# One list-scheduled attention and MLP kernel: filler matmuls at the start, score pieces two by two, batch-0 transposes in separate PSUM slots, and two v tiles ahead of the rest

## The chip, the cores and the metric

The kernel runs on one core of a Trainium2 chip. The metric is device time in microseconds (us), the lower the better. A kernel is timed in several executions; medians are quoted. A ratio is the mean time of one kernel's fast runs over the mean of the other's fast runs in the same rounds, so it is not quite the ratio of the medians quoted beside it. The record's verdict on a kernel is "faster" or "slower" only where the ratio is clear of 2%.

## The reference, cut to what matters

```python
B, H, S, Nb, D = 8, 8, 576, 16, 64          # batches, heads, tokens, beacon keys, head size
k_all = concat([beacon_k, k], axis=2); v_all = concat([beacon_v, v], axis=2)
scores = q @ k_all.T / sqrt(D)              # causal mask on the non-beacon keys
x = softmax(scores) @ v_all                 # -> (B*S, H*D) = (4608, 512)
h = x @ w_in                                # (512, 2048)
out = (relu(h) ** 2) @ w_out                # (2048, 512)
```

Eight batches of attention feed one two-layer MLP. The MLP works on nine chunks of 512 tokens. A batch has 576 tokens, so chunk 3 (tokens 1536 to 2047) needs the first 320 tokens of batch 3, and chunk 4 needs the first 256 of batch 4. Batches and chunks are counted from 0.

## The kernel before

The kernel is not written as a loop. Its Python code makes a list of operations with dependences, priorities and assumed durations, plays them on a small model of the engines, and emits the instructions in the order that comes out. Only the order enters the program. Each engine gets its list in that order, with semaphore waits for the dependences. In what follows "the plan" is that list scheduler.

PSUM is cut into four slots. Each operation that writes PSUM takes one, with a limit for each class:

```python
order = Order(pools={"ps": range(4), "stg": range(NSTG), "pt": range(NPT)},
              limits={"strip": 2, "av": 2, "mlp": 2, "tp": 1})
# in Order.run: an operation is not issued while its class is at its limit or no slot is free
```

A head pair's scores are made in four pieces in the batches after the first (batch 0 is cut differently). Each piece takes one slot, and one ScalarE exponential empties it:

```python
for i, (mms, off, width) in enumerate(ph.pieces):
    ...
    qk = add(f"qk{p}.{n}.{i}", "PE", 0.05 + cols / 2400.0, emit_qk, prio=base + i,
             deps=qk_deps + [take_pt], take=("ps", "strip"), gate=gate)
    ...
    exps.append(add(f"exp{p}.{n}.{i}", "ACT", 0.18 + 2 * width / 1200.0, emit_exp,
                    prio=base + i, deps=[qk], give=qk))
```

Score matmuls contract over 64 rows, and those of two heads run side by side (in the trace of before their starts are 0.003 us apart); value matmuls and MLP matmuls use 128 rows (64*128 against 128*128 in the timeline). After masking, the value matmuls and the normalisation write `xn`, the attention output of a batch. For batches 2 to 7 five DMA transposes per batch turn it into `xT`, which the MLP reads. They are issued on SyncE's queue, together with the fp32 loads of later batches, the q/k transposes of batches 3 to 7 and the stores.

```python
def add_trans(b, x, prio):        # q/k transposes of batch b, on SyncE
    ...
    deps = [cast[b, x, c] for c in range(NT)]                       # all loads cast
    deps += [o for p in range(HP * (b - 2), HP * (b - 1)) for o in qk_ops[p]]   # qT/kT buffer free
    trans[b, x] = [add(f"tr{b}{x}", "SP", 3.8, emit, prio=prio, deps=deps, dma=3.2)]

def add_xt(b):                    # xT of batch b, on SyncE
    for t in range(NT):
        ...
        deps = [norm_ops[HP * b + i, 0] for i in range(HP)] + ring_deps(tok, tok + n)
        o = add(f"xt{b}.{t}", "SP", 1.32, emit, prio=-50.0 + b, deps=deps, dma=0.64 * n / 128)
```

At the start, batch 0's q and k are loaded pair by pair and transposed on TensorE, k and q of a pair into one slot. VectorE copies k out and ScalarE or VectorE q. The v tiles are loaded after the first q has landed, and the MLP's weights after v tile 3.

The softmax here doesn't subtract the row's maximum and nothing guards it: scores larger than these inputs give would overflow.

## Time and profile before

| reading | value | where it is read |
|---|---|---|
| time, median | 355.3 us (354.6 to 355.4) | timed runs |
| TensorE busy | 334.7 of 353.2 us | busy table of the page |
| first MLP matmul, last matmul ends | 27.61, 348.49 us | timeline |
| first exponential | 10.15 us | timeline |
| TensorE waits over 0.9 us after the start | one, 1.0 us | list of waits |

From the page of the kernel before: the busy table, and the rows of TensorE, ScalarE and the granted TensorE clock in 40 slices of the span, each digit a share in tenths.

```profile
PE 334.7 (95%) x2943; PEld 178.6 (51%) x2980; DVE 148.9 (42%) x287; ACT 193.4 (55%) x233; POOL 85.5 (24%) x132
...
PE   3789999999999989999999999999999999999994
...
ACT  2686786287555764665745663676634405505602
...
PEclk9999999999999999999999999999999999999999
```

TensorE is nearly always busy after the third slice. The clock row reads full throughout, but the timeline of all engines says otherwise for the first 23 us. Its columns are start, time, engine, source line, operation, output and input.

```profile
4.63 1.43 PE L405 MATMUL ps<-ident,qk_area 96*64 96x96 bf16 x24 [0.24 <-DMA qk_area<-in_k_dram]
...
10.15 1.54 ACT L520 ACTIVATE pt<-ps 128x736 bf16<-128x736 f32 x2
...
27.61 0.99 PE L678 MATMUL ps<-xT,w_in 128*128 128x240 bf16 x8
...
34.61 0.70 PE L405 MATMUL ps<-ident,qk_area 96*64 96x96 bf16 x24
```

The same 24 transposes take 1.43 us at 4.6 us (a wait of up to 0.24 us for the q load is in it; the next pair's take 1.31 us) and 0.70 us at 34.6 us, so TensorE starts at about half its later speed. The first exponential starts at 10.15 us and the first MLP matmul at 27.61 us.

The list of waits of TensorE (what it waited for, total us, times, longest):

```profile
PE ps L401 <- DVE bks L373: 4.2, 1, 4.2
...
PE ps L506 <- DMA kT<-qk_area: 1.0, 1, 1.0
PE ps L550 <- DVE pt L530: 0.9, 1, 0.9
...
PE ps L678 <- ACT qT L280: 0.6, 1, 0.6
```

After the start there is one wait of 1.0 us for the key transposes of batch 4 (at 129 us) and one of 0.6 us.

A score island (a run of score or transpose matmuls between others; it has two edges, entry and exit), in TensorE's timeline:

```profile
203.53 1.91 PE L678 MATMUL ps<-xT,w_in 128*128 128x256 bf16 x16
205.37 0.58 PE L506 MATMUL ps<-qT,kT 64*128 64x496 bf16 x4
205.88 1.38 PE L678 MATMUL ps<-xT,w_in 128*128 128x256 bf16 x11
```

Sixteen matmuls of 256 columns start 0.109 us apart, which is 1.744 us. The scores start 1.84 us after the first of them, so 0.096 us is lost on entering. Leaving costs about the same: 0.09 us, the median of 68 exits in this trace.

### The profile page before, as it was taken

Reading aid. Unit: us, or ns where it says so; the run is one execution under the profiler, and the core shown is the slowest. Engines: PE = TensorE matmul, PEld = TensorE weight load, DVE = VectorE, ACT = ScalarE, POOL = GpSimd, SP = SyncE. Lnnn points to the kernel's source line nnn. Section 1 sums busy time; section 2 is a strip of 40 time slices with the busy share of each in tenths; the row PEclk is TensorE's granted clock in tenths of the full one; section 3 lists DMA queues with packets and bytes.
Section 4 is the critical chain, followed back from the end, with each engine's and each line's share of the span. In section 5 each row is a group of like instructions: output and inputs, shape, how many; then the busy total and the mean of one; then the engine's idle time right before and its main releaser. Section 6 shows DMA issues by size and latency. Waiting matters only on the chain.

```text
span 353.2 us, 7173 instructions
## 1 busy us (share of the span) xinstructions
PE 334.7 (95%) x2943; PEld 178.6 (51%) x2980; DVE 148.9 (42%) x287; ACT 193.4 (55%) x233; POOL 85.5 (24%) x132
## 2 busy tenths in 40 slices
PE   3789999999999989999999999999999999999994
PEld 2459665554545444444446874445454444444441
DVE  5576674349714455146622753247132302301300
ACT  2686786287555764665745663676634405505602
POOL 7273721209215504133501651000000000000000
PEclk9999999999999999999999999999999999999999
DMA  7999999965969999699989999440013103003003
GB/s 101 183 160 204 223 206 211 201 169 118 206 116 236 223 221 191 138 224 222 251 137 202 248 213 209 115 118 11 0 61 69 59 0 121 0 0 121 0 0 119
DMA packets 137008, 49.49 MB, mean 140 GB/s; under 512 B 123344, under 2 KB 132048, under 8 KB 136976
## 3 DMA queue, kind: packets, MB, share of 16 engines
q1 hardware_dynamic: 127472, 40.09, 53.4%
q0 software_dynamic: 9504, 8.95, 15.7%
q8 instruction: 23, 0.38, 0.5%
q14 instruction: 9, 0.07, 0.1%
HBM read 37.22 MB, written 9.44 MB: 132 GB/s over the span
## 4 chain that ended last, share of the span: by engine, by line
PE 74%; DMA 12%; SPq 5%; ACT 4%; DVE 2%; issue 2%; POOL 1%; ACTq 0%; DVEq 0%; POOLq 0%
PE ps L678 32%; PE ps L718 27%; PE ps L550 7%; PE ps L506 6%; DMA stg<-in_k_dram 4%; DMA stg<-in_v_dram 4%; SPq L597 3%; ACT pt L520 2%; DMA kT<-qk_area 2%; DMA stg<-in_q_dram 1%; SPq L327 1%; DVE kT L282 1%; DMA qk_area<-in_q_dram 1%; PE ps L405 1%; ACT qT L280 1%
## 5 line engine op out<-in xcount | busy, mean ns | idle before, releaser
L678 PE MATMUL ps<-xT,w_in 128*128 128x512 bf16 (+3 forms) x689 | 131.9, 340 | 1.6 <-ACT qT L280 0.6
L718 PE MATMUL ps<-w_out,g 128*128 128x512 bf16 x554 | 129.5, 380 | 1.4 <-issue 0.5
L520 ACT ACTIVATE pt<-ps 128x832 bf16<-128x832 f32 (+4 forms) x128 | 105.3, 865 | 40.7 <-PE ps L506 40.2
L678 PEld LDWEIGHTS <-w_in 128*128 128x128 bf16 x704 | 66.0, 98 | 57.6 <-issue 6.0
L694 ACT ACTIVATE g<-ps 128x1024 bf16<-128x1024 f32 (+2 forms) x65 | 61.8, 951 | 54.0 <-PE ps L678 53.8
L718 PEld LDWEIGHTS <-g 128*128 128x128 bf16 x576 | 53.0, 98 | 65.7 <-issue 5.8
L703 DVE TENSOR_TENSOR g<-g 128x1024 bf16<-128x1024 bf16 (+2 forms) x80 | 53.0, 664 | 77.5 <-ACT g L694 77.0
L530 DVE TENSOR_TENSOR pt<-pt,tri 128x1024 bf16<-128x1024 bf16 (+1 forms) x36 | 24.8, 692 | 50.1 <-ACT pt L520 48.6
L282 POOL CAST qk_area<-stg 128x512 bf16<-128x512 f32 (+2 forms) x50 | 34.6, 704 | 35.0 <-DMA stg<-in_k_dram 18.7
L282 POOL CAST vb<-stg 128x512 bf16<-128x512 f32 (+1 forms) x38 | 26.0, 695 | 69.6 <-DMA stg<-in_v_dram 59.1
L506 PE MATMUL ps<-qT,kT 64*128 64x80 bf16 (+6 forms) x400 | 39.1, 291 | 1.7 <-DMA kT<-qk_area 1.0
L280 ACT COPY osb<-ps 128x1024 f32<-128x1024 f32 (+1 forms) x19 | 18.3, 969 | 40.6 <-PE ps L718 40.3
L550 PEld LDWEIGHTS <-pt 128*128 128x128 bf16 (+1 forms) x960 | 34.5, 99 | 8.8 <-issue 2.5
L550 PE MATMUL ps<-vb,pt 128*128 128x65 bf16 (+1 forms) x960 | 36.5, 196 | 1.9 <-DVE pt L530 0.9
L566 DVE TENSOR_TENSOR xn<-ps,rcp 128x640 bf16<-128x640 f32 (+2 forms) x36 | 27.0, 750 | 1.7 <-DMA xT<-xn 0.4
L506 PEld LDWEIGHTS <-kT 64*128 64x128 bf16 x400 | 13.7, 97 | 24.2 <-issue 18.8
L565 DVE RECIPROCAL rcp<-ps 128x10 f32<-128x10 f32 (+2 forms) x36 | 7.6, 211 | 38.1 <-PE ps L550 36.2
L696 DVE TENSOR_SCALAR g<-ps 128x1024 bf16<-128x1024 f32 (+2 forms) x15 | 15.8, 1053 | 7.8 <-PE ps L678 7.0
L280 ACT COPY qT<-ps 128x576 bf16<-128x576 bf16 x12 | 7.7, 640 | 16.1 <-DVE kT L282 13.0
L282 DVE COPY kT<-ps 128x16 bf16<-128x16 bf16 (+1 forms) x24 | 9.9, 456 | 9.7 <-PE ps L405 7.5
L405 PE MATMUL ps<-ident,qk_area 96*64 96x96 bf16 x288 | 11.1, 233 | 2.9 <-DMA qk_area<-in_k_dram 1.8
L534 DVE TENSOR_TENSOR pt<-pt,tri 80x160 bf16<-80x160 bf16 x32 | 10.8, 339 | 0.0
(31 smaller groups left out, 57.1 us busy)
## 6 DMA issues: line engine op xcount, KB each, us to landing
out_dram<-osb SPq DMA_DIRECT2D x17, 512.0 KB, 3.5
stg<-in_v_dram SPq DMA_DIRECT2D x21, 256.0 KB, 5.1
stg<-in_q_dram SPq DMA_DIRECT2D x20, 256.0 KB, 4.8
stg<-in_k_dram SPq DMA_DIRECT2D x15, 256.0 KB, 5.1
w_in<-in_moe_w_in_dram POOLq DMA_DIRECT2D x4, 512.0 KB, 8.2
w_out<-in_moe_w_out_dram POOLq DMA_DIRECT2D x4, 512.0 KB, 10.6
stg<-in_v_dram SPq DMA_DIRECT2D x7, 224.0 KB, 4.7
qk_area<-in_k_dram POOLq DMA_DIRECT2D x4, 288.0 KB, 12.4
```

What stands on the lines that cost most here:

```text
L280: nc.scalar.copy(dst, src)
L282: eng[e].tensor_copy(dst, src)
L506: nc.tensor.matmul(st[:, hj, at:at + t1 - t0], kT[b % 2][hp, pr, 128 * c:128 * c + 128], qT[b % 2][hp, pr, t0:t1], start=True, stop=True,)
L520: nc.scalar.activation(pt[take_pt.held[2]][:, :, off:off + width], st[:, :, 0:width], AF.Exp, bias=0.0, scale=scale)
L530: nc.vector.tensor_tensor(out=d, in0=d, in1=tri[:, m0:m0 + m, :][:, None].to_broadcast([128, 2, m, 128]), op=ALU.min)
L550: nc.tensor.matmul(a[:, hj, (t - tl[0]) * (D + 1):(t - tl[0] + 1) * (D + 1)], P[0:rr, hj, o:o + 128], vb[b % 2][0:rr, c, h, :], start=(c = ...
L566: nc.vector.tensor_tensor(out=xn[b % 2].rearrange("p t (h d) -> p h t d", d=D)[:, 2 * pr:2 * pr + 2, tl[0]:tl[0] + nt], in0=a[:, :, :, 0:D ...
L678: nc.tensor.matmul(h[:, u, lo - spans[0][0]:hi - spans[0][0]], w_in_sb[:, mc, ft * 128:(ft + 1) * 128], xT[:, mc, lo % RING:lo % RING + hi ...
L694: nc.scalar.activation(dst, h, AF.Relu, bias=0.0, scale=1.0)
L696: nc.vector.tensor_scalar(out=dst, in0=h, scalar1=0.0, scalar2=None, op0=ALU.max)
L703: nc.vector.tensor_tensor(out=d, in0=d, in1=d, op=ALU.mult)
L718: nc.tensor.matmul(o[:, ts, :], G[:, fc, (2 * u + ts) * 128:(2 * u + ts + 1) * 128], w_out_sb[:, fc, :], start=(fc == 0), stop=(fc == NFT ...
```

## The change

It has four parts. The first three are meant to bring the first MLP unit forward; the last is meant to save changes between MLP and score matmuls (0.096 us on entering in the trace of before).

1. Filler matmuls on TensorE, into the slot that the next operation will use, wherever the plan has a gap before the first MLP unit: 79 in all, 40 of them before the first transpose.
2. In batch 0, k and q of a pair are transposed into slots of their own, and ScalarE alone copies q. (The class limit of these transposes becomes 2, for all batches.)
3. v tiles 0 and 1 are loaded at once; tiles 2 to 4 wait for the third pair's q; the weights wait for v tile 2 instead of 3.
4. In batches 3 to 7 score pieces are made two by two: one operation takes two PSUM slots and issues both pieces back to back; the two exponentials give the slots back one at a time. The assumed duration of a score operation gains 0.12 us, in all batches.

The diff, cut to its core:

```diff
-                            pool, cls = op.take
-                            if not self.pools[pool]:
+                            pool, cls, n = op.take if len(op.take) == 3 else op.take + (1,)
+                            if len(self.pools[pool]) < n:
                                 continue
-                            if cls in self.limits and self.inuse[cls] >= self.limits[cls]:
+                            if cls in self.limits and self.inuse[cls] + n > self.limits[cls]:
                                 continue
 ...
+    filler = pt[NPT - 1][:, 0, 1920:2048]
+    nc.vector.memset(filler, 0.0)
+    def keep_busy(slot, gap):
+        for _ in range(int((gap - 0.15) / 0.07)):
+            nc.tensor.matmul(ps[slot][:, 0, 0:128], filler, filler, start=True, stop=True)
 ...
+            for part in (("k", "q") if b == 0 else ("kq",)):
 ...
+    QGROUP = lambda b: 1 + (b >= 3)
 ...
-        for i, (mms, off, width) in enumerate(ph.pieces):
+        for i in range(0, len(ph.pieces), QGROUP(b)):
+            group = ph.pieces[i:i + QGROUP(b)]
 ...
-            qk = add(f"qk{p}.{n}.{i}", "PE", 0.05 + cols / 2400.0, emit_qk, prio=base + i,
-                     deps=qk_deps + [take_pt], take=("ps", "strip"), gate=gate)
+            qk = add(f"qk{p}.{n}.{i}", "PE", 0.17 + cols / 2400.0, emit_qk, prio=base + i,
+                     deps=qk_deps + [take_pt], take=("ps", "strip", len(group)), gate=gate)
 ...
-            w_ops["in", i] = add(... sync=[v_loads[0][3]] if i == 0 else (), ...)
+            w_ops["in", i] = add(... sync=[v_loads[0][2]] if i == 0 else (), ...)
 ...
-                if c == 0:
-                    sync = [strided[0][0, "q"]]
+                if c == 2:
+                    sync = [strided[0][2, "q"]]
```

More of the change, by code (lines that the diff above doesn't have):

```diff
@@ L21 @@
                  "take", "give", "gate", "held", "dma", "pe_time", "behind", "followers",
-                 "sync", "insts")
+                 "sync", "insts", "fill", "idx")
     def __init__(self, name, engs, dur, emit, prio=0.0, deps=(), take=None, give=None,
-                 gate=None, dma=0.0, pe_time=0.0, behind=(), sync=()):
+                 gate=None, dma=0.0, pe_time=0.0, behind=(), sync=(), fill=None):
         self.name = name
@@ L41, in __init__ @@
         self.followers = []
+        self.fill = fill
+        self.idx = []
 class Order:
@@ L97, in run @@
                 elif kind == "give":
-                    pool, cls, idx = op.give.held
-                    self.pools[pool].append(idx)
+                    owner, k = op.give if isinstance(op.give, tuple) else (op.give, 0)
+                    pool, cls = owner.held[:2]
+                    self.pools[pool].append(owner.idx[k])
                     if cls in self.inuse:
@@ L139, in run @@
                     if op.take:
-                        pool, cls = op.take
-                        op.held = (pool, cls, self.pools[pool].pop(0))
+                        pool, cls, n = op.take if len(op.take) == 3 else op.take + (1,)
+                        op.idx = [self.pools[pool].pop(0) for _ in range(n)]
+                        op.held = (pool, cls, op.idx[0])
                         if cls in self.inuse:
-                            self.inuse[cls] += 1
+                            self.inuse[cls] += n
                     dur = op.dur[e] if isinstance(op.dur, dict) else op.dur
@@ L165, in run @@
         assert len(issued) == len(self.ops), [o.name for o in self.ops if id(o) not in started][:20]
-        for op, e, _ in issued:
+        busy_to = 0.8
+        warming = True
+        for op, e, at in issued:
+            if e == "PE":
+                warming = warming and op.pe_time == 0.0
+                if warming and op.take:
+                    self.keep_busy(op.idx[0], at - busy_to)
+                busy_to = max(busy_to, at + op.dur)
             if e != "-":
@@ L249 @@
         pools={"ps": range(4), "stg": range(NSTG), "pt": range(NPT)},
-        limits={"strip": 2, "av": 2, "mlp": 2, "tp": 1},
+        limits={"strip": 2, "av": 2, "mlp": 2, "tp": 2},
     )
     order.wait_for = wait_for
+    filler = pt[NPT - 1][:, 0, 1920:2048]
[3 more added lines that the diff above has]
+            nc.tensor.matmul(ps[slot][:, 0, 0:128], filler, filler, start=True, stop=True)
+    order.keep_busy = keep_busy
     add = order.add
@@ L396, in add_strided @@
             h = slice(2 * pr, 2 * pr + 2)
-            box = {}
-            def emit_tp(e, pr=pr, h=h, box=box):
-                pp = ps[box["t"].held[2]].bitcast(BF16)
-                nc.tensor.transpose(pp[:, 1, 0:Nb], bks[b % 2][:, h, :], ident[0:Nb, 0:Nb])
-                for half, at, t in ((1, Nb, ks), (0, 0, qs)):
-                    for u in range(NS):
-                        for hj in range(2):
-                            nc.tensor.transpose(pp[64 * hj:64 * hj + 64, half, at + u * NP:at + (u + 1) * NP],
-                                                t[b % 2][:, 2 * pr + hj, u, :], ident[0:NP, 0:NP])
@@ L408, in add_strided @@
-            busy = qk_ops[HP * (b - 2) + pr] if b >= 2 else []
-            tp = add(f"tp{b}.{pr}", "PE", 0.8 if b else 1.3, emit_tp, prio=100.0 * (HP * b + pr) - 190,
-                     deps=[bk, loads[pr, "k"], loads[pr, "q"], ident_op] + busy, take=("ps", "tp"))
-            box["t"] = tp
-            def emit_k(e, pr=pr, box=box):
-                pp = ps[box["t"].held[2]].bitcast(BF16)
-                copy_on(e, kT[b % 2][:, pr, 0:Nb], pp[:, 1, 0:Nb])
-                copy_on(e, kT[b % 2][:, pr, Nb:Nb + S].rearrange("p (n s) -> p n s", s=NS),
-                        pp[:, 1, Nb:Nb + S].rearrange("p (s n) -> p n s", s=NS))
@@ L419, in emit_q @@
-            def emit_q(e, pr=pr, box=box):
-                pp = ps[box["t"].held[2]].bitcast(BF16)
-                copy_on(e, qT[b % 2][:, pr, 0:S].rearrange("p (n s) -> p n s", s=NS),
-                        pp[:, 0, 0:S].rearrange("p (s n) -> p n s", s=NS))
-            ek = add(f"ek{b}.{pr}", "DVE", 0.9, emit_k, prio=-200.0, deps=[tp])
-            eq = add(f"eq{b}.{pr}", ("DVE", "ACT"), 0.75, emit_q, prio=-199.0, deps=[tp])
-            add(f"tpg{b}.{pr}", "-", 0.0, None, prio=0.0, deps=[ek, eq], give=tp)
@@ L427, in add_strided, with emit_tp, emit_k, emit_q @@
-            trans[b, "k"].append(ek)
-            trans[b, "q"].append(eq)
+            busy = qk_ops[HP * (b - 2) + pr] if b >= 2 else []
+            boxes = {}
+            for part in (("k", "q") if b == 0 else ("kq",)):
+                def emit_tp(e, pr=pr, h=h, boxes=boxes, part=part):
+                    pp = ps[boxes[part].held[2]].bitcast(BF16)
+                    if "k" in part:
+                        nc.tensor.transpose(pp[:, 1, 0:Nb], bks[b % 2][:, h, :], ident[0:Nb, 0:Nb])
+                    for x, half, at, t in (("k", 1, Nb, ks), ("q", 0, 0, qs)):
+                        if x in part:
+                            for u in range(NS):
+                                for hj in range(2):
+                                    nc.tensor.transpose(pp[64 * hj:64 * hj + 64, half, at + u * NP:at + (u + 1) * NP],
+                                                        t[b % 2][:, 2 * pr + hj, u, :], ident[0:NP, 0:NP])
+                tp = add(f"tp{b}.{pr}{part}", "PE", 0.2 + 0.35 * len(part), emit_tp,
+                         prio=100.0 * (HP * b + pr) - 190 + (5 if part == "q" else 0),
+                         deps=[bk, ident_op] + [loads[pr, x] for x in part] + busy, take=("ps", "tp"))
+                def emit_k(e, pr=pr, boxes=boxes, part=part):
+                    pp = ps[boxes[part].held[2]].bitcast(BF16)
+                    copy_on(e, kT[b % 2][:, pr, 0:Nb], pp[:, 1, 0:Nb])
+                    copy_on(e, kT[b % 2][:, pr, Nb:Nb + S].rearrange("p (n s) -> p n s", s=NS),
+                            pp[:, 1, Nb:Nb + S].rearrange("p (s n) -> p n s", s=NS))
+                def emit_q(e, pr=pr, boxes=boxes, part=part):
+                    pp = ps[boxes[part].held[2]].bitcast(BF16)
+                    copy_on(e, qT[b % 2][:, pr, 0:S].rearrange("p (n s) -> p n s", s=NS),
+                            pp[:, 0, 0:S].rearrange("p (s n) -> p n s", s=NS))
+                boxes[part] = tp
+                ev = []
+                if "k" in part:
+                    ev.append(add(f"ek{b}.{pr}", "DVE", 0.9, emit_k, prio=-200.0, deps=[tp]))
+                    trans[b, "k"].append(ev[-1])
+                if "q" in part:
+                    ev.append(add(f"eq{b}.{pr}", ("DVE", "ACT") if b else "ACT", 0.75, emit_q, prio=-199.0, deps=[tp]))
+                    trans[b, "q"].append(ev[-1])
+                add(f"tpg{b}.{pr}{part}", "-", 0.0, None, prio=0.0, deps=ev, give=tp)
@@ L496, in add_phase, with emit_qk @@
         exps = []
-        for i, (mms, off, width) in enumerate(ph.pieces):
-            cols = sum(max(96, t1 - t0) for _, t0, t1, _ in mms)
+        for i in range(0, len(ph.pieces), QGROUP(b)):
+            group = ph.pieces[i:i + QGROUP(b)]
+            cols = sum(max(96, t1 - t0) for mms, _, _ in group for _, t0, t1, _ in mms)
             box = {}
-            def emit_qk(e, mms=mms, box=box):
-                st = ps[box["qk"].held[2]]
-                for c, t0, t1, at in mms:
-                    for hj in range(2):
-                        hp = slice(64 * hj, 64 * hj + 64)
-                        nc.tensor.matmul(
-                            st[:, hj, at:at + t1 - t0],
-                            kT[b % 2][hp, pr, 128 * c:128 * c + 128],
-                            qT[b % 2][hp, pr, t0:t1],
-                            start=True, stop=True,
-                        )
-            qk = add(f"qk{p}.{n}.{i}", "PE", 0.05 + cols / 2400.0, emit_qk, prio=base + i,
-                     deps=qk_deps + [take_pt], take=("ps", "strip"), gate=gate)
+            def emit_qk(e, group=group, box=box):
+                for at_ps, (mms, _, _) in zip(box["qk"].idx, group):
+                    st = ps[at_ps]
+                    for c, t0, t1, at in mms:
+                        for hj in range(2):
+                            hp = slice(64 * hj, 64 * hj + 64)
+                            nc.tensor.matmul(
+                                st[:, hj, at:at + t1 - t0],
+                                kT[b % 2][hp, pr, 128 * c:128 * c + 128],
+                                qT[b % 2][hp, pr, t0:t1],
+                                start=True, stop=True,
+                            )
+            qk = add(f"qk{p}.{n}.{i}", "PE", 0.17 + cols / 2400.0, emit_qk, prio=base + i,
+                     deps=qk_deps + [take_pt], take=("ps", "strip", len(group)), gate=gate)
@@ L515, in add_phase, with emit_exp @@
             box["qk"] = qk
             qk_ops[p].append(qk)
-            def emit_exp(e, off=off, width=width, box=box):
-                st = ps[box["qk"].held[2]]
-                nc.scalar.activation(pt[take_pt.held[2]][:, :, off:off + width], st[:, :, 0:width],
-                                     AF.Exp, bias=0.0, scale=scale)
-            exps.append(add(f"exp{p}.{n}.{i}", "ACT", 0.18 + 2 * width / 1200.0, emit_exp, prio=base + i,
-                            deps=[qk], give=qk))
+            for m, (_, off, width) in enumerate(group):
+                def emit_exp(e, off=off, width=width, box=box, m=m):
+                    st = ps[box["qk"].idx[m]]
+                    nc.scalar.activation(pt[take_pt.held[2]][:, :, off:off + width], st[:, :, 0:width],
+                                         AF.Exp, bias=0.0, scale=scale)
+                exps.append(add(f"exp{p}.{n}.{i + m}", "ACT", 0.18 + 2 * width / 1200.0, emit_exp, prio=base + i + m,
+                                deps=[qk], give=(qk, m)))
@@ L641, in emit @@
                     in_=moe_w_in.rearrange("(m p) f -> p m f", p=128)[:, :, i * w:(i + 1) * w])]
-            w_ops["in", i] = add(f"win{i}", "POOL", 1.3, emit, prio=-100 + i, sync=[v_loads[0][3]] if i == 0 else (),
+            w_ops["in", i] = add(f"win{i}", "POOL", 1.3, emit, prio=-100 + i, sync=[v_loads[0][2]] if i == 0 else (),
                                  behind=[w_ops["in", i - 1]] if i else (), dma=3.15)
```

## The prediction

> **What bounds it now.** The busy table gives TensorE 334.7 of 353.2 us. From its first MLP matmul (27.6 us, timeline) to its last (348.1 us) the list of TensorE waits is short: 1.0 us at 129 us for the key transposes, 0.6 us near 44 us for the q eviction. So a gain must be an earlier first MLP unit or less TensorE work after it.
>
> Before 27.6 us no engine is full. TensorE starts at 4.2 us and is slow: 24 k/q transposes take 1.31 to 1.43 us, against 0.70 us at 34.6 us; 24 attention-value matmuls take 1.52 us at 22.6 us, 0.89 us at 24.8 us. The speed changes near 23 us. The page's clock row reads full throughout; the durations say otherwise. [...] ScalarE's first exponential starts at 10.15 us, the last of batch 0 ends at 28.6 us; about 15.2 us of that is busy (windows).
>
> **The change.**
> 1. Filler: 79 matmuls, 40 ahead of the first transpose, the rest in gaps, all before the first MLP unit. [...]
> 2. Split k/q slots in batch 0: now ScalarE's q copy waits for VectorE's k copy (7.03 after 6.93 us). Side by side, and with score pieces ahead of the next pair's transposes, the first exponential should come at 7.5 to 9 us.
> 3. v tiles 0-1 first: 512 KB compete with the first k/q loads (landing 4.6 and 5.3 us), perhaps 1 us later; later k/q loads come earlier. The weights wait for v tile 2, not 3; their issue moves from 17.4 to about 14 us.
> 4. Scores two by two: entering or leaving the two-row-tile matmuls costs 0.096 us (MLP to score starts 0.312 us apart against 0.216 us; score to MLP 0.131 after an 80-column matmul that streams in about 0.035). [...] In program order, score/transpose islands after the first MLP unit fall from 72 to 60: 24 edges, 2.3 us, all critical. Half of the PSUM slots must be free at once; I allow 0.5 us of new waits.
>
> **Sum.** Exponentials begin about 2 us earlier and idle less (3.3 us idle now): first MLP unit at about 25 us, minus 2.7 us. Edges minus 2.3. The 129 us wait goes, as scores stand later against the MLP: minus 1. New waits plus 0.5. Together about minus 5.5 us.
>
> **Predicted: 349.8 us, 8 in 10 between 345.5 and 353.5.** Faster by over 2% 0.30, within 2% 0.68, slower 0.02.
>
> **What would show it.** Pair 0's 24 transposes at 0.7 us; first exponential 7.5 to 9 us; first weight issue 13 to 15 us; first MLP matmul 24.5 to 26 us; TensorE's stretch from first to last MLP matmul 317 to 319 us, against 320.5 us; edges still 0.096 us; no new TensorE wait over 0.5 us.
>
> **What would make it wrong.** The clock stays cold, or fillers delay the first transposes; v loads delay k/q by over 2 us; the first MLP unit waits for w_in; two-slot scores stall TensorE or hold ScalarE before the MLP's evictions; attention ends about one chunk later, so the last MLP chunks may wait for the last batch's transposes.

The sum came to minus 2.7, minus 2.3, minus 1 and plus 0.5, together minus 5.5 us, from 355.3 to 349.8 us. What the trace of before shows is the slow start itself (24 transposes in 1.31 to 1.43 us, against 0.70 us at 34.6 us); the "cold" clock in the prediction's last paragraph means that.

## More of the kernel before

SyncE's queue around the issue of xT of batch 3 (the time is that of the issue, with any wait in it):

```profile
134.13 1.09 SPq L327 DMA_DIRECT2D stg<-in_k_dram  x1
135.31 7.11 SPq L597 DMA_TRANSPOSE xT<-xn  x5
142.52 1.99 SPq L327 DMA_DIRECT2D stg<-in_q_dram  x1
```

The last normalisation of batch 3 in VectorE's timeline, and the first matmuls of chunk 3 in TensorE's:

```profile
128.12 0.82 DVE L566 TENSOR_TENSOR xn<-ps,rcp 128x640 bf16<-128x640 f32 x1
...
151.61 1.90 PE L678 MATMUL ps<-xT,w_in 128*128 128x512 bf16 x8
```

xT of batch 3 was ready at 128.9 us (end of its last normalisation), was issued from 135.31 us, and the three tiles that chunk 3 needs had landed at 141.0 us. Chunk 3's first matmul started at 151.61 us, without a wait. So 10.6 us were to spare.

## The result, and the profile after

The changed kernel took 360.06 us (median of 4, 359.53 to 361.91) against 355.18 us in the same rounds: ratio 1.015, 95% interval 1.011 to 1.019. It is 1.5% slower, clear of noise though inside 2%, and the time lies outside the predicted range.

The page of the changed kernel, the same rows:

```profile
PE 339.7 (94%) x3059; PEld 181.8 (50%) x3059; DVE 152.5 (42%) x295; ACT 186.2 (52%) x228; POOL 82.8 (23%) x130
...
PE   6999999999999999199997999999999999999995
...
ACT  1996785766444544066443753575457504604502
...
PEclk9999999999999999789998999999999999999999
```

There is a hole in TensorE's row at slice 17, counted from 1 (144 to 153 us), and the clock is below full in slices 17, 18 and 22. The start, in the timeline of all engines, looks as intended:

```profile
3.43 4.45 PE L269 MATMUL ps<-pt 128*128 128x128 bf16 x40 [3.43 <-DVE pt L281]
...
7.93 0.83 PE L427 MATMUL ps<-ident,qk_area 96*64 96x96 bf16 x24
...
9.96 2.47 ACT L548 ACTIVATE pt<-ps 128x736 bf16<-128x736 f32 x3 [0.51 <-PE ps L534]
...
24.63 0.99 PE L706 MATMUL ps<-xT,w_in 128*128 128x240 bf16 x8
```

Filler runs from 3.43 us, the 24 transposes of pair 0 take 0.83 us, and the first MLP matmul starts at 24.63 us, 2.98 us earlier than before. The list of TensorE's waits has a new first line:

```profile
PE ps L706 <- DMA xT<-xn: 10.4, 2, 7.7
PE ps L269 <- DVE pt L281: 3.4, 1, 3.4
PE ps L746 <- ACT qT L299: 0.5, 1, 0.5
```

TensorE waited 10.4 us for xT, in two waits of 7.7 and 2.7 us. The first one in its timeline:

```profile
142.10 1.90 PE L746 MATMUL ps<-w_out,g 128*128 128x512 bf16 x8
151.68 3.52 PE L706 MATMUL ps<-xT,w_in 128*128 128x512 bf16 x8 [7.68 <-DMA xT<-xn]
...
155.54 1.90 PE L746 MATMUL ps<-w_out,g 128*128 128x512 bf16 x8
```

TensorE comes to the MLP of chunk 3 at 143.8 us and starts it at 151.68 us. Its first eight matmuls then take 3.52 us; the eight of the same size at 142.10 us took 1.90 us. The trace's clock record is at half from 148.19 to 155.02 us, and again from 192.56 to 195.98 us, after the second wait. The second drop lasts 3.41 us, the first twice that. The first began 4.2 us into its wait; the second followed a wait of only 2.7 us.

Why was xT late? VectorE's timeline shows when the last normalisation of batch 3 was done (133.68 + 0.82 = 134.5 us):

```profile
133.68 0.82 DVE L594 TENSOR_TENSOR xn<-ps,rcp 128x640 bf16<-128x640 f32 x1
```

SyncE's queue shows what it did with it:

```profile
131.24 6.05 SPq L346 DMA_DIRECT2D stg<-in_v_dram  x5
137.38 0.63 SPq L345 DMA_DIRECT2D stg<-in_beacon_k_dram  x1
138.06 0.42 SPq L346 DMA_DIRECT2D stg<-in_k_dram  x1
138.58 3.77 SPq L378 DMA_TRANSPOSE qT<-qk_area  x1
142.44 3.33 SPq L378 DMA_TRANSPOSE kT<-qk_area  x1
145.82 0.58 SPq L346 DMA_DIRECT2D stg<-in_q_dram  x1
146.49 6.43 SPq L625 DMA_TRANSPOSE xT<-xn  x5
```

xT of batch 3 was ready at 134.5 us and was issued at 146.49 us. In between, the queue worked off a run of v loads, a k load, the q and k transposes of batch 5 (3.77 and 3.33 us of issue) and a q load. In the kernel before, xT of batch 3 stood ahead of those transposes.

The account of the profiled runs (the one of the changed kernel was the slowest of its four, 361.91 us; by medians the loss is 4.9 us): 360.2 minus 353.2 us is 7.0 us. The start gave 3.0. The stretch from the first MLP matmul to the end of the last matmul grew from 320.9 to 331.1 us, by 10.2: plus 10.7 of excess between matmul starts at the two waits (7.84 and 2.86), plus about 3.4 at half clock (half of the 3.34 and 3.41 us that TensorE worked so), and so minus 3.9 for the rest. An estimate for the profiled run without waits and half clock is 361.9 - 14.1 = 347.8 us, 2.0 us under the forecast. It assumes that nothing else would have filled that time.

### The profile page after: what moved, and what is told of

Its sections match the earlier page's. It is cut to its first block, busy times and chain, and to the rows that moved or that the text cites. A ratio compares the mean times of both kernels' runs of the same rounds, so it can differ in the third digit from the quotient of the medians.

```text
span 360.2 us, 7353 instructions
## 1 busy us (share of the span) xinstructions
PE 339.7 (94%) x3059; PEld 181.8 (50%) x3059; DVE 152.5 (42%) x295; ACT 186.2 (52%) x228; POOL 82.8 (23%) x130
## 4 chain that ended last, share of the span: by engine, by line
PE 77%; DMA 7%; SPq 7%; DVE 3%; ACT 3%; POOL 1%; issue 1%; ACTq 0%; POOLq 0%; DVEq 0%
PE ps L706 32%; PE ps L746 28%; PE ps L578 7%; PE ps L534 6%; SPq L625 3%; DMA stg<-in_k_dram 3%; PE ps L269 2%; SPq L378 2%; DMA stg<-in_v_dram 2%; PE ps L427 2%; SPq L346 1%; ACT pt L548 1%; DMA xT<-xn 1%; DVE kT L301 1%; DMA stg<-in_q_dram 1%
## 5 line engine op out<-in xcount | busy, mean ns | idle before, releaser
L706 PE MATMUL ps<-xT,w_in 128*128 128x512 bf16 (+3 forms) x704 | 136.0, 346 | 10.8 <-DMA xT<-xn 10.4
L746 PE MATMUL ps<-w_out,g 128*128 128x512 bf16 x576 | 131.9, 380 | 0.5 <-ACT qT L299 0.5
L731 DVE TENSOR_TENSOR g<-g 128x1024 bf16<-128x1024 bf16 (+2 forms) x80 | 51.7, 649 | 100.2 <-ACT g L722 99.9
L722 ACT ACTIVATE g<-ps 128x1024 bf16<-128x1024 f32 (+2 forms) x59 | 56.1, 950 | 73.3 <-PE ps L706 73.3
L301 POOL CAST vb<-stg 128x512 bf16<-128x512 f32 (+1 forms) x36 | 24.0, 692 | 64.2 <-DMA stg<-in_v_dram 31.4
L578 PEld LDWEIGHTS <-pt 128*128 128x128 bf16 (+1 forms) x960 | 33.2, 97 | 7.4 <-issue 2.0
L534 PE MATMUL ps<-qT,kT 64*128 64x80 bf16 (+5 forms) x400 | 36.2, 280 | 0.0
L724 DVE TENSOR_SCALAR g<-ps 128x1024 bf16<-128x1024 f32 (+2 forms) x21 | 22.7, 1079 | 14.5 <-PE ps L706 13.9
L534 PEld LDWEIGHTS <-kT 64*128 64x128 bf16 x400 | 12.4, 95 | 21.4 <-issue 17.3
L269 PE MATMUL ps<-pt 128*128 128x128 bf16 x79 | 8.1, 267 | 4.0 <-DVE pt L281 3.4
L562 DVE TENSOR_TENSOR pt<-pt,tri 80x160 bf16<-80x160 bf16 x32 | 10.4, 325 | 0.0
```

What stands on the lines that cost most here:

```text
L301: eng[e].tensor_copy(dst, src)
L534: nc.tensor.matmul(st[:, hj, at:at + t1 - t0], kT[b % 2][hp, pr, 128 * c:128 * c + 128], qT[b % 2][hp, pr, t0:t1], start=True, stop=True,)
L578: nc.tensor.matmul(a[:, hj, (t - tl[0]) * (D + 1):(t - tl[0] + 1) * (D + 1)], P[0:rr, hj, o:o + 128], vb[b % 2][0:rr, c, h, :], start=(c = ...
L706: nc.tensor.matmul(h[:, u, lo - spans[0][0]:hi - spans[0][0]], w_in_sb[:, mc, ft * 128:(ft + 1) * 128], xT[:, mc, lo % RING:lo % RING + hi ...
L722: nc.scalar.activation(dst, h, AF.Relu, bias=0.0, scale=1.0)
L724: nc.vector.tensor_scalar(out=dst, in0=h, scalar1=0.0, scalar2=None, op0=ALU.max)
```

## The experiments

Two things had changed around xT: its place on SyncE's queue, and the time at which the MLP asks for it. In the program order, the MLP matmuls that stand between the last value matmuls of a batch and the chunk that needs it fell from 80, 88, 136, 104 and 136 (batches 3 to 7) to 40, 32, 32, 32 and 32. With single pieces and all else as in the changed kernel (e2_single below) they are 80, 96, 144, 96 and 144, so it is the pairs that put attention later and MLP earlier. A likely reason, which no run isolates: a score pair can only be issued when two PSUM slots are free at once, while an MLP unit takes any single one.

- Queue theory: the wait is made by what stands ahead of xT on SyncE's queue.
- Lateness theory: pairing finishes attention too late for the MLP, whatever the queue's order.
- A third: the earlier start makes TensorE outrun the loads.

In the tables "ready" is the end of a batch's last normalisation, "issued" the first xT issue, "landed" the landing of the third tile, the last one that the chunk needs, and "asked" the moment when TensorE would have gone on. "TensorE waits" is the excess between its matmul starts there, which is a little more than the idle time in its list of waits. All are read from the trace's instructions.

### xT ahead on the queue (e1_xt_first)

```diff
+        names = [op.name for op, _, _ in issued]
+        for b in (3, 4, 5):
+            for x in "qk":
+                at, to = names.index(f"tr{b + 2}{x}"), names.index(f"xt{b}.4")
+                if at < to:
+                    issued.insert(to, issued.pop(at))
+                    names.insert(to, names.pop(at))
```

The plan is made first and only the emitted order on SyncE is edited, so every other engine keeps its list.

> The changed kernel, with nothing but the order on the DMA-issuing queue (SyncE) edited: the xT transposes of batches 3, 4 and 5 stand ahead of the q/k transposes of batches 5, 6 and 7 instead of behind them. Queue theory (xT of batch 3 was ready for issue at 134.5 us but stood behind about 7.2 us of q/k transposes until 146.5 us): the 7.8 us TensorE stall at 144 us shrinks to under 1 us, the 2.9 us stall at 189 us goes, the clock does not drop to half after them, and the time is 348 us (346.5 to 349.5). Lateness theory (score pairs bring attention too late for the MLP whatever the queue's order): a stall of 3 us or more stays near 144 us and the time stays above 354 us.

Measured: 354.67 us (354.27 to 355.26), ratio 0.998. The first wait shrank from 7.8 to 0.9 us, and its half clock went. But a wait of 4 us stayed at the next chunk, with 3.41 us at half clock after it. From TensorE's timeline of this kernel:

```profile
180.92 0.60 PE L713 MATMUL ps<-xT,w_in 128*128 128x256 bf16 x4
185.41 1.38 PE L713 MATMUL ps<-xT,w_in 128*128 128x256 bf16 x7 [3.89 <-DMA xT<-xn]
```

So the queue's order is worth 5.4 us, and it is not all. xT of batch 4 was ready at 173.3 us and issued at 179.5 us, behind loads (four of them hold the queue for 6.31 us from 170.05 us); it landed at 185.3 us and was asked for at 181.4 us. Neither theory was met whole: the queue theory said 348 us and no wait; the lateness theory said over 354 us, which came, with a wait of 3 us or more near 144 us, which did not.

### Single score pieces (e2_single)

```diff
-    QGROUP = lambda b: 1 + (b >= 3)
+    QGROUP = lambda b: 1
```

> The changed kernel with score pieces one by one again in batches 3 to 7; filler, split slots and v order stay. On the queue the q/k transposes of batch 5 still stand ahead of xT of batch 3, but the last value matmuls of batch 3 stand 80 MLP matmuls ahead of the chunk that needs them, not 40. If the order on the queue alone makes the stall, it stays (4 us or more near 150 us, time over 356 us). If the stall is queue lateness (about 9 us against the planned order, in both kernels) minus the lead that pairing takes away, there is no stall over 1 us, and what is left is the start: first MLP matmul at 24.6 us and 352 us (351 to 353.5).

Measured: 349.56 us (349.10 to 349.85), ratio 0.984. No wait over 1 us, and no half clock after the start. The queue is as slow as in the changed kernel:

```profile
136.39 4.34 SPq L378 DMA_TRANSPOSE qT<-qk_area  x1
140.82 3.20 SPq L378 DMA_TRANSPOSE kT<-qk_area  x1
144.12 6.54 SPq L625 DMA_TRANSPOSE xT<-xn  x5
```

xT of batch 3 was ready at 127.8 us and issued at 144.12 us, 16 us later, behind the same transposes. It landed at 149.3 us. TensorE asked at 150.01 us, 0.7 us after. So most of xT's lateness is not the pairs' doing: it lands nearly as late without them (151.5 us with them, 141.0 us before the change). Their part is that TensorE asks 6.2 us sooner. The time was 2.4 us better than expected: the stretch from the first MLP matmul to the last was 318.5 us, 2.4 us shorter than before. Two things in the trace come to about that: the plan itself had put more single pieces side by side (65 score and transpose islands against 72, so 14 edges or 1.3 us), and the wait of 1.0 us at 129 us had gone.

### Reverse order in the kernel before (e3_before_xt3_late)

```diff
+        for x in range(5):
+            at, to = names.index(f"xt3.{x}"), names.index("tr5k")
+            if at < to:
+                issued.insert(to, issued.pop(at))
+                names.insert(to, names.pop(at))
```

> The kernel before, with nothing but the queue's order edited: xT of batch 3 behind the q/k transposes of batch 5. Issue of xT moves from 135 us to about 150 us or later, data 5 us after. Queue theory: a TensorE stall of 3 to 7 us appears before the first MLP matmul of chunk 3 (151.6 us in the profile of before), then some us at half clock; time 358 to 363 us. Lateness theory (pairing alone does it): no stall, 355 us.

Measured: 366.30 us (365.47 to 366.61), ratio 1.030. The only new long wait of TensorE is 8.8 us for xT from 152.8 us:

```profile
161.62 3.57 PE L684 MATMUL ps<-xT,w_in 128*128 128x512 bf16 x8 [8.82 <-DMA xT<-xn]
```

The clock is at half for 10.2 us, from 154.93 to 165.17 us; 3.6 us of that lie after the wait. xT of batch 3 was ready at 129.5 us and issued at 153.8 us. The queue's order alone can make the wait, without pairs and without the new start. The size was underestimated (11 us against 3 to 8).

### Pairs alone (e4_pairs_only)

The changed kernel with filler off, joint k/q slots and the old v order (the diffs of the three start runs below, together). The class limit of 2 and the longer assumed durations stay.

> The changed kernel with the start put back (no filler, joint k/q slots, old v order), so only the score pieces two by two. If pairing costs the time, the stalls near 144 to 150 us and 190 us are there (together 6 us or more) and the time is 360 to 365 us, about 3 us over the changed kernel, whose start it lacks. If the earlier start brought the stalls (TensorE too early for the loads), they shrink by the 3 us of the start and the time is about 356 to 358 us.

Measured: 361.10 us (360.73 to 362.90), ratio 1.018. First MLP matmul at 28.46 us; waits for xT of 6.2 us at chunk 3 and 0.7 us at chunk 4, 6.8 us at half clock. The third theory falls: the waits come with the pairs, without the early start. But the early start adds to them: the first wait was 1.4 us and the second 2.0 us shorter than with it. Of the 3.8 us by which the changed kernel's first MLP matmul comes sooner than here, 1.0 us is left in the time.

### xT on ScalarE's queue (e9_xt_act)

```diff
-                nc.sync.dma_start(out=xT[:, :, at:at + n], in_=xn[b % 2][0:n, t, :], transpose=True)
+                nc.scalar.dma_start(out=xT[:, :, at:at + n], in_=xn[b % 2][0:n, t, :], transpose=True)
```

> The changed kernel, score pairs and all, with the xT transposes issued from ScalarE's queue instead of SyncE's; nothing else edited. If SyncE's queue is what makes xT late, xT of batch 3 is issued when its last normalisation ends (134.5 us) or within 2 us and has landed by about 141 us, before TensorE asks for it (143.7 us); both stalls go, no half clock, and SyncE's loads come earlier too: 346 to 349.5 us. ScalarE pays about 1.26 us of issue for each of 30 transposes, which may give back 1 to 3 us where it holds an exponential or an eviction. If attention itself is too late for the MLP, stalls of over 3 us stay near 144 and 181 us and the time is over 353 us.

Measured: 355.86 us (355.55 to 357.29), ratio 1.003. Both waits for xT are gone with all pairs in place: xT of batch 3 was ready at 134.3, issued at 134.4 and landed at 142.6 us; xT of batch 4 was ready and issued at 172.0 and landed at 179.9 us. Chunk 3 started at 143.72 us and chunk 4 came to batch 4 at 180.0 us, so attention was not too late for the MLP, but at chunk 4 with hardly anything to spare. The time was missed for another reason, a new wait of 5.1 us at 212 us, with 6.8 us at half clock. ScalarE's timeline there:

```profile
213.58 1.20 ACTq L625 DMA_TRANSPOSE xT<-xn  x1
214.88 0.86 ACT L548 ACTIVATE pt<-ps 128x832 bf16<-128x832 f32 x1 [9.08 <-issue]
```

ScalarE stood still for 9 us in front of an exponential, because the xT issue ahead of it waited. The k transpose of batch 6 on SyncE's queue landed at 213.44 us, and the issue came at 213.58 us. The trace has that wait as a semaphore instruction of ScalarE, which stood for 9.28 us; from that landing to the issue it is 0.14 us. Why the wait is there no run shows. In this run, then, the transposes on the second queue were not free of those on the first.

### Pairs in fewer batches (e10_pairs_6_7 and e11_pairs_5_7)

```diff
-    QGROUP = lambda b: 1 + (b >= 3)
+    QGROUP = lambda b: 1 + (b >= 6)     # e10;  b >= 5 for e11
```

> Score pieces two by two in batches 6 and 7 only, with the whole new start. xT of batches 6 and 7 never waits on the queue in any run so far, and TensorE asks for chunks 3 and 4 as late as with single pieces (150.0 and 186.4 us). No stall over 1 us; 62 score islands against 65: 0.6 us less than single pieces, about 349 us (348 to 350).

> Pairs in batches 5 to 7. Attention of batch 4 ends as early as with single pieces, but the MLP's chunk 4 stands earlier in TensorE's order, about 7 us by the plan (179 us instead of 186). If the supply of xT of batch 4 is set by SyncE's queue (landed 186.8 us with single pieces, 20 us after it was ready), a stall of 3 to 7 us appears at chunk 4 alone, none at chunk 3, and the time is 352 to 357 us. If late attention makes the stalls, there is none, because attention of batch 4 is not later: 349 us.

Measured: e10 348.48 us (348.33 to 349.05), ratio 0.982, no wait over 1 us. e11 356.51 us (355.30 to 357.44), ratio 1.004, with one wait, at chunk 4, and 6.8 us at half clock. TensorE's timeline of e11:

```profile
180.06 0.60 PE L706 MATMUL ps<-xT,w_in 128*128 128x256 bf16 x4
185.37 1.89 PE L706 MATMUL ps<-xT,w_in 128*128 128x256 bf16 x8 [4.71 <-DMA xT<-xn]
```

Attention of batch 4 is not later in e11 than in e10 (ready at 159.4 and 159.8 us), and xT landed at nearly the same time (185.3 and 186.0 us), 26 us after it was ready. What moved is the asking: pairs in batch 5 pushed batch 5's attention behind chunk 4's MLP matmuls, so chunk 4 asked at 180.5 us instead of 187.0. This separates the two: xT arrives when SyncE's queue gets to it, and pairing makes the MLP ask sooner.

### The queue's order with one early chunk (e14_q5_xt_first), and with the scatter (e15_q6_xt_first)

e14 is e11, and e15 is e10, with the queue edit of the first experiment for batches 3 and 4 only.

> Pairs in batches 5 to 7 (356.5 us, a 4.7 us wait at chunk 4, whose xT was ready at 159.4 us and issued at 180.3 us, behind the q/k transposes of batch 6), with only the queue's order edited: xT of batches 3 and 4 ahead of the q/k transposes of batches 5 and 6. If the queue's order makes the wait, xT of batch 4 is issued near 171 us and has landed by 177 us, before TensorE asks (180.6 us): no wait, no half clock, 348 to 349 us. If TensorE's early arrival at chunk 4 cannot be met by the queue whatever its order, a wait of over 2 us stays.

> Pairs in batches 6 and 7 with the filler as in the changed kernel (348.5 us, spread 0.7 us), and only the queue's order edited as in the run beside it. If the scatter of the two kernels with early filler (348.5 to 353.0 us) comes from the early filler, this one stays within 1 us around 348.5 us. If it comes from the queue's order, it scatters by 2 us or more.

Measured: e14 348.41 us (347.78 to 349.03), ratio 0.980 (0.978 to 0.982): 8.1 us less than e11 by medians, from the order of transposes on one queue. xT of batch 4 was issued at 170.75 us:

```profile
170.75 8.11 SPq L632 DMA_TRANSPOSE xT<-xn  x5
178.96 3.01 SPq L385 DMA_TRANSPOSE kT<-qk_area  x1
...
179.77 1.91 PE L713 MATMUL ps<-xT,w_in 128*128 128x256 bf16 x16
```

It landed at 178.1 us, and chunk 4 ran through without a wait from 179.77 us (last line, TensorE). This is the fastest median of all, level with e10 (348.48 us, measured on another chip).

e15: 350.12 us (348.50 to 350.50), ratio 0.984. Here the q/k transposes of batch 6, which now stand behind xT, are the ones that come late: TensorE waited 1.2 us ahead of the first scores of batch 6 at 191.7 us. The expectation for this run offered two causes of scatter; it scattered by 2.0 us without the early filler, which speaks for the queue's order, but four runs do not settle it. Where nobody waited for xT, the same edit made the kernel 1.6 us slower by medians.

Supply and demand of the chunks, in us:

| kernel | chunk | ready | issued | landed | asked | TensorE waits |
|---|---|---|---|---|---|---|
| before | 3 | 128.9 | 135.3 | 141.0 | 151.6 | none |
| changed | 3 | 134.5 | 146.5 | 151.5 | 143.8 | 7.8 |
| changed | 4 | 181.5 | 186.7 | 192.3 | 189.6 | 2.9 |
| e1, xT first | 3 | 134.9 | 138.3 | 144.8 | 144.2 | 0.9 |
| e1, xT first | 4 | 173.3 | 179.5 | 185.3 | 181.4 | 4.0 |
| e2, single | 3 | 127.8 | 144.1 | 149.3 | 150.0 | none |
| e11, pairs 5-7 | 4 | 159.4 | 180.3 | 185.3 | 180.5 | 4.9 |
| e14, and xT first | 4 | 159.1 | 170.8 | 178.1 | 180.2 | none |

### The three parts of the start (s1_no_filler, s2_no_split, s3_old_v)

Each takes one part away from e2_single (349.56 us, first MLP matmul at 24.44 us).

```diff
# s1_no_filler
-    order.keep_busy = keep_busy
+    order.keep_busy = lambda slot, gap: None
# s2_no_split
-            for part in (("k", "q") if b == 0 else ("kq",)):
+            for part in ("kq",):
# s3_old_v
-            w_ops["in", i] = add(... sync=[v_loads[0][2]] if i == 0 else (), ...)
+            w_ops["in", i] = add(... sync=[v_loads[0][3]] if i == 0 else (), ...)
-                if c == 2:
-                    sync = [strided[0][2, "q"]]
+                if c == 0:
+                    sync = [strided[0][0, "q"]]
```

> Single pieces with the new start but no filler matmuls. TensorE's transposes of pair 0 take 1.3 us or more per 24 again and its clock turns full only near 20 us. First MLP matmul at 26 to 27 us instead of 24.4 us, time 351 to 352 us: filler is then worth about 2 us. If ScalarE and the loads set the start, it stays below 25.2 us and the time within 0.7 us of 349.6 us.

> Single pieces with filler and the new v order, but k and q transposes of a batch-0 pair share one PSUM slot as before. If the split gives most of the start's 3 us, the first exponential comes 1 us or more later than 9.5 us, the first MLP matmul at 26 us or later, and the time is 351 to 352 us against 349.6. If the v and weight order gives it, the first MLP matmul stays within 0.7 us of 24.4 us.

> Single pieces with filler and split slots, but the old v order (v after the first q load, weights after v tile 3). The first k and q loads land earlier (4.6 and 5.3 us instead of 5.4 and 7.8 us), the later ones later (the last at about 13.9 us instead of 12.3 us). If that order matters, the first MLP matmul is at 25.4 us or later and the time about 350.5 us; weights are issued at about 17 us and land at about 22.7 us, still before they are needed, so I expect less: within 1 us of 349.6 us.

| kernel | first exponential | first MLP matmul | time (range) |
|---|---|---|---|
| e2_single | 9.51 | 24.44 | 349.56 (349.10 to 349.85) |
| s1_no_filler | 8.66 | 25.38 | 349.86 (349.51 to 349.97) |
| s2_no_split | 10.83 | 27.22 | 352.46 (351.74 to 352.58) |
| s3_old_v | 10.27 | 26.19 | 352.68 (350.46 to 353.24) |

Read the two columns of single moments with care, since each is from one profiled run: eight kernels here (the changed one, e1, e2, e9, e10, e11, e14 and e15) have the same start in their programs, and their first exponential lies between 9.02 and 10.30 us, their first MLP matmul between 23.70 and 24.98 us. Filler is worth little: 0.3 us by medians, within the ranges, though without it the clock record turns full only at 21.6 us (24 value matmuls take 1.50 us at 17.9 us and 0.89 us at 22.6 us). It starts at 3.43 us (its operand lies in a buffer that VectorE clears until then) and in the changed kernel holds the first transposes back until 7.8 us, when the first k had landed at 5.4 us and the first q at 7.0 us (4.6 and 5.3 us in the kernel before). In e2 it ended at 7.2 us and the first q landed only at 7.8 us, so there the load came last. The split is worth 2.9 us. The v order is worth 3.1 us by medians (with a range of 2.8 us), more than I expected, and part of it is not at the start: with the old order, small waits for xT appeared at chunks 3 and 4 (0.8 and 0.9 us), and the clock fell to half from 14.2 to 17.6 us, although no gap on TensorE there reached 0.7 us. The parts do not add up, since each run is a new plan.

### Earlier filler (e12_own_filler), and with the queue edit (e13_best)

```diff
# both, on top of e10
-    filler = pt[NPT - 1][:, 0, 1920:2048]
+    filler = g[1][:, 0, 0:128]
# e13 also has the queue edit of the first experiment for batches 3 and 4
```

> Pairs in batches 6 and 7 (348.5 us), with the filler's operand in a buffer whose only early write is its own clearing, so that filler starts near 1.1 us instead of 3.43 us (there it waited for the clearing of the whole buffer) and ends by about 5.5 us instead of 7.7 us, near the landing of the first k. Clock full at about 6 us or earlier as before, first exponential at 8.7 us or earlier instead of 9.7 us, first MLP matmul 0.5 to 1 us earlier than 24.3 us, time 347.5 to 348.3 us. If the first transposes wait for their loads and not for the filler, nothing changes.

> The version with pairs in batches 6 and 7 and the early filler (349.0 to 353.0 us, first MLP matmul 23.55 us), with xT of batches 3 and 4 ahead of the q/k transposes of batches 5 and 6 on SyncE's queue. In that version chunk 4 asked for xT of batch 4 at about the moment it landed (0.8 us wait in the profile, some 4 us in two of its four runs, if that is the cause of their spread). If the queue's supply is the limit, xT of batches 3 and 4 lands some 6 us earlier, no wait at 187 us, the spread falls under 1 us and the time is 347 to 348.3 us. The q/k transposes of batches 5 and 6 come some 6 us later; they had 12 and 7 us to spare, so a wait of up to 1 us before the scores of batch 6 (190 us) may appear. If the spread has another cause it stays at 3 us or more.

Measured: e12 350.96 us (348.99 to 352.96), ratio 0.989; e13 349.75 us (348.54 to 351.74, 6 runs), ratio 0.986. The first MLP matmul came at 23.55 and 23.62 us, 0.7 to 0.8 us earlier than in e10 (but only 0.1 us before the earliest of the eight above), and the time did not follow. In e12's profile chunk 4 waits 0.6 us for xT, which landed at 187.5 us, 1.5 us later than in e10, and was asked for at nearly the same moment (186.8 against 187.0 us). In e13's profile that wait is gone, yet its scatter of 3.2 us stays, which its expectation counted as another cause. Its two slowest runs have a mean granted clock of 0.98 against 0.99 to 1.00; of e12's two slow ones, one has 0.98 and the other 1.00. Where in those runs the clock was low is not recorded, and the scatter is left open. So e10 or e14 is the version to keep.

## Why the prediction was wrong

- **First MLP unit 2.7 us earlier: right.** It came 2.98 us earlier in the two profiled runs. Single runs of one start differ by about 1 us (23.70 to 24.98 us above; 28.47 us in e3, whose program starts as the kernel before does, at 27.61 us), so the size is good to that. The stated course held in part: the first exponential came at 9.96 us, not 7.5 to 9 us; filler held the first transposes back to 7.8 us, though k and q had landed by 7.0 us. The clock was full from 8.2 us by its record.
- **24 edges at 0.096 us, 2.3 us: in size consistent, not isolated.** After the change an edge still costs 0.096 us (median in the trace), and the islands fell from 72 to 60 as planned. The stretch without waits and half clock came out 3.9 us shorter than before, which holds this term and the next.
- **The 129 us wait goes, 1 us: right in the trace.** It is absent after. But its reason, "scores stand later against the MLP", is not shown: in e2, without pairs, the wait is gone too. And that scores stand later is the same fact that helped to make the loss. I booked it as a gain only.
- **"New waits plus 0.5": this is the step that failed.** In its place stand 10.7 us of waits and about 3.4 us at half clock. I looked for them at the PSUM slots. There they did not appear. They came where attention feeds the MLP. Chunk 3 was asked for at 143.8 us instead of 151.6, while xT landed at 151.5 us instead of 141.0. Both sides of a 10.6 us reserve were used up, 7.8 us by earlier asking and 10.5 us by later landing. The later landing is there without the pairs (e2: 149.3 us) and without the new start (e4: 154.1 us); in both, the plan had put xT behind the q/k transposes of batch 5. Which of the changed limits and assumed durations did that was not isolated. The pairs brought the earlier asking. Without them 0.7 us of reserve was left, and that it was enough is luck.
- **The risk was named in the wrong place.** The prediction's last sentence feared it for the last chunks. The runs show no wait there: xT of batches 5 to 7 landed 3 to 4 us before its chunk started. The waits were at chunks 3 and 4, where SyncE's queue still carries loads and q/k transposes.

Shown by runs: with the new plan's queue order, the pairs in batches 3 to 5 cause the loss (e2: 10.5 us less by medians without any; e10: none with pairs in batches 6 and 7 only; e4: the loss without the new start). Shown: it works through SyncE's queue (e3, e9, e14). Shown: attention's own lateness is not needed (e11 waits at chunk 4 with attention early, ready at 159.4 us; e9 does not wait for xT at chunk 3 with attention late, ready at 134.3 us, though xT landed only 1.1 us before chunk 3 started). Why the queue runs late against its loads was not tested; in the trace of the changed kernel five load issues in a row take 6.05 us at 131 us, while single ones take 0.42 us at 138 and 156 us and 0.37 us at 178 us.

## What to carry to other kernels

When a change reorders work between a producer and a consumer, look up the reserve at each hand-over (landed to asked, in the trace of before), not only the waits that exist: a reserve of 10 us looks like nothing in a list of waits. Here a late issue queue decided when data landed, whatever the data's own readiness (xT of batch 4 in e11: ready at 159.4 us, issued at 180.3, landed at 185.3), so put what the next consumer needs ahead of what is wanted later: one swap on such a queue was worth 8.1 us here (e14 against e11), more than the change's intended gain, and cost 1.6 us where nobody was waiting (e15 against e10). Making a producer's work coarser in a list scheduler can shift the order of everything: look at the new order before believing the gain.

## What these traces show of the hardware

- An entry to the two-row-tile score matmuls cost 0.096 us at full clock, in both traces (512-column MLP matmul to score 0.312 us, against 0.216 us to the next such matmul); an exit cost 0.09 us (median of 68 in the trace of before).
- In the changed kernel an idle time of 2.7 us (2.97 us between two matmul starts) was followed by 3.41 us at half clock, and the 256-column matmuls in it started 0.213 us apart instead of 0.109. In the waits of 5 to 9 us (changed, e3, e4, e9, e11) half clock began 2.1 to 4.2 us after the last matmul had ended and outlasted the wait by 3.3 to 5.0 us, so by estimate (half of the latter) each such wait cost 1.7 to 2.5 us on top of itself, where TensorE was busy throughout.
- A DMA transpose held the issuing queue, with any wait in it, for 1.26 us (median) for an xT tile and 3.1 to 4.1 us for the q or k of a batch, in the changed kernel. The five xT tiles of batch 3 were issued there from 146.49 to 151.68 us and landed from 149.68 to 154.03 us.
- With xT's transposes on ScalarE's queue, ScalarE's exponential stood 9.1 us behind such an issue (e9).
- For reading the profile: the clock row showed full where there was no record yet, before 24.3 us in the kernel before. The durations (1.31 to 1.43 against 0.70 us for the same transposes) are what showed the slow start.
